# Weight sums moved from Pool to VectorE, one tile's statistics to ScalarE, transposes ahead of loads, in a fused attention and GLU kernel

## Chip, cores, metric

The kernel runs on one core of a Trainium2 chip. The metric is device time in microseconds (us) for one execution; a time quoted for a kernel is the median of its runs. Runs of one kernel lie within about 0.3% of each other. The comparisons below use five rounds, and the trace of one profiled run of each kernel to see where time went. In the views PE is TensorE (matmuls), PEld its weight loads, DVE VectorE, ACT ScalarE, POOL Pool and SPq the queue that issues transfers; a bank is a part of PSUM, the memory that TensorE writes its results to, and PEclk or granted clock is the share of its full clock that TensorE was given.

## The reference, cut to what matters

```python
h  = x + A_ref(layernorm(x), wqkv, wo)      # linear attention, S=2048, D=1024, 32 heads
h2 = h + B_ref(layernorm(h), W_gate, W_up, W_down)   # gate*relu-mask*up, F=3584
# A_ref: q, k, v = x @ wqkv;  phi(t) = where(t > 0, t + 1, exp(t)) + 1e-6
#        kv = sum_s phi(k) v;  o = phi(q) kv / (phi(q) z);  return o @ wo
```

Only the first 125 us of the kernel matter here: layer norm of x and the products for k, v and q.

## The kernel before

The rows of x come in 16 tiles of 128. Each is normalized, transposed (tiles 0 to 3 on TensorE, later ones by DMA) and multiplied with the weights. From the tiles 0 and 1 on for keys, and from tiles 6 and 7 on for values, a pair of tiles is multiplied by a Strassen-like scheme with seven products instead of eight. It needs sums of weight blocks (`w_sums`, four per matrix, computed once) and sums of x blocks (`x_sums`, four per pair of tiles). The first values are plain products (`v_piece`). A queue of each engine is filled in program order by `PL.add`, with semaphores worked out from buffers read and written.

```python
def x_sums(p):                       # four 512-column sums per pair of tiles, VectorE
    ...
    add(2, xb(0, 0), xb(0, 1), ALU.subtract, ...)      # read by product P7, the second one
    add(0, xb(0, 1), xb(1, 1), ALU.add, ...)
    add(1, s(0), xb(0, 0), ALU.subtract, ...)          # read by P6, the third one
    add(3, xb(1, 0), s(1), ALU.subtract, ...)

# start of the program, tiles 1 to 5 (cut)
v_piece(0, 0, lambda: T1(1))         # T1(t): the eight TensorE transposes of tile t
v_piece(1, 0, lambda: T1(2))
x_sums(0)
ln1_norm(3)
pool_q += w_sums("pool", wv_, bw_v, tw_v, B_TWv, "TWv", 1, NW // 2)    # values: 32 pieces
v_piece(2, 0, lambda: T1(3))
v_piece(0, 1)
twk = w_sums("dve", wkv, bw_k, tw_k, B_TWk, "TWk", KH)                 # keys: 4 sums
...
pool_q += w_sums("pool", wq, bw_q, TWq, B_TWq, "TWq", 1, NW // 2)      # queries: 32 pieces
...
# hooks of a key group: pieces of Pool work, statistics of the tiles to come
def k1():
    pool_piece(2)
    if A < NST:
        ln1_stats(A)                 # VectorE
def k5():
    pool_piece(2)
    if B < NST:
        m_, q_ = ln1_stats_act(B)    # ScalarE
        ...
# the group of seven products, in the order of TensorE (cut)
#   P1, P7 (x sum 3), P6 (x sum 2), P2, P5 (x sum 1), P4, P3 (x sum 4); ScalarE copies a bank
#   after P1 (needed by P6) and after P6 (needed by P5), VectorE and ScalarE finish the results
```

In the profiles L804 of the kernel before (L800 after) is `w_sums`, L829 (L825) `x_sums`, L739 (L733) and L673 norms, L688, L691 and L907 (L903) the finishing of keys, L616 every matmul, L754 (L748) the transposes on TensorE, L630 to L637 statistics on VectorE, L654 and L659 statistics on ScalarE, L640 and L662 to L668 the norms' small root steps on Pool.

## Time and profile before

| | before |
|---|---|
| time, median of the runs made with the prediction's result | 751.87 us |
| TensorE busy | 739.3 us (99%) |
| VectorE busy | 538.4 us (72%) |
| Pool busy | 89.9 us (12%) |
| TensorE time lost, 12 to 15 us | 0.92 us |
| TensorE time lost, 43.5 to 53 us | 3.49 us |

"Time lost" is worked out from the trace: the distance between the starts of consecutive matmuls, less 0.213 us for 512 columns (in proportion for fewer); the median distance is 0.216 us, so a little of every matmul counts as lost. Some traces lack 56 of the 3,595 matmul records; a missing record looks like 0.213 to 0.219 us lost, and I took those out, but not in the half-clock stretches below, where each matmul loses 0.213 us and none is missing (as many matmuls as weight loads). The first 12 us are left out of comparisons, because their loss ranged from 2.8 to 4.2 us between profiled runs with the arrival of the first loads.

The page of the kernel before, busy time by engine and Pool's busy tenths in 40 slices of the span:

```profile
PE 739.3 (99%) x3595; PEld 335.1 (45%) x3595; DVE 538.4 (72%) x1063; ACT 308.0 (41%) x532; POOL 89.9 (12%) x152
...
POOL 2985620000360000000000010000000000000000
```

TensorE is the bound, so only its idle time can be won. The chain for tile 3, from the timeline of the kernel before (start, duration, engine, line; in brackets the idle time before and who ended it):

```profile
12.21 0.75 DVE L829 TENSOR_TENSOR RWG<-RAB 128x512 f16<-128x512 bf16 x2
...
13.80 0.54 DVE L673 TENSOR_SCALAR RXH<-RE,mv,rstd 128x1024 bf16<-128x1024 bf16 x1
14.39 0.45 PEld L754 LDWEIGHTS ps<-ident,RXH 128*128 128x128 bf16 x8 [1.22 <-DVE RXH L673]
14.39 0.62 PE L754 MATMUL ps<-ident,RXH 128*128 128x128 bf16 x8 [0.73 <-DVE RXH L673]
```

The norm L673 stands behind the x sums L829, and TensorE waits for it. The larger loss, from VectorE's and Pool's timelines of the kernel before:

```profile
25.59 8.21 POOL L804 TENSOR_TENSOR RW<-RAB 128x256 f16<-128x256 bf16 x10
...
38.02 10.87 POOL L804 TENSOR_TENSOR RW<-RAB,RW 128x256 f16<-128x256 bf16 x14
```

```profile
34.60 0.76 DVE L688 TENSOR_SCALAR RX<-RX 128x512 bf16<-128x512 bf16 x1
...
41.43 0.78 DVE L829 TENSOR_TENSOR RWG<-RWG,RAB 128x512 f16<-128x512 f16 x1
42.24 0.77 DVE L829 TENSOR_TENSOR RH<-RAB,RWG 128x512 f16<-128x512 bf16 x1
42.94 1.27 DVE L630 BATCH_NORM_STATS2 st<-RE 128x6 f32<-128x512 bf16 x2
...
47.02 1.34 DVE L829 TENSOR_TENSOR RWG<-RAB 128x512 f16<-128x512 bf16 x2
48.40 0.77 DVE L829 TENSOR_TENSOR RWG<-RWG,RAB 128x512 f16<-128x512 f16 x1
```

The wait itself, from the timeline of the kernel before:

```profile
47.70 1.02 PE L616 MATMUL ps<-RW,RWG 128*128 128x512 f16 x4 [2.20 <-DVE RWG L829]
```

And the waits view of the kernel before for 40 to 50 us (who waited for whom, us in total, times, longest):

```profile
PEld ps L616 <- POOL RW L804: 2.7, 1, 2.7
PE ps L616 <- DVE RWG L829: 2.2, 1, 2.2
```

The view names two culprits for one gap, before the second product of the first value group. The Pool sum that this product reads is the first of the four, 8 of the 32 pieces, and four pieces ran before the ten shown from 25.59 us; the eighth ended near 29 us. The x sum, the other operand, started at 47.02 us. So the question is why VectorE was late; its operations beside Pool's take 0.76 to 0.78 us where 0.29 (L688) and 0.42 us (L829) are their usual times.

### The profile page before, as it was taken

The page shows a single profiled execution, that of the slowest core. Times are in us where ns is not written, and L with a number is a line of the kernel's source. Part 1 is how long each engine was busy: PE and PEld are TensorE (multiplying, and loading weights), DVE is VectorE, ACT ScalarE, POOL GpSimd, SP SyncE. Part 2 cuts the span into 40 slices and gives each one's busy share as a digit, 9 for nine tenths or more (in the row PEclk, how much of TensorE's full clock was granted, in tenths as well). Part 3 has the DMA queues.
Part 4 walks back from the last instruction along what each step waited for, and adds up shares of the span by engine and source line. Part 5 has one row for each costly group of instructions (what it writes and reads, how often), then busy time and mean ns, then how long its engine had stood idle before and what let it go on. Part 6 is the DMA issues. An engine that isn't in the chain of part 4 may idle for free.

```text
span 750.0 us, 10163 instructions
## 1 busy us (share of the span) xinstructions
PE 739.3 (99%) x3595; PEld 335.1 (45%) x3595; DVE 538.4 (72%) x1063; ACT 308.0 (41%) x532; POOL 89.9 (12%) x152
## 2 busy tenths in 40 slices
PE   8989999999999999999999999999999999999998
PEld 3434444344554444444444444444444444444443
DVE  7797856889776799888877494856868677563343
ACT  4657755664842354545453100035454454520000
POOL 2985620000360000000000010000000000000000
PEclk9999999999999999999999999999999999999999
DMA  9624135013998796665537799733324241035764
GB/s 303 201 58 113 28 97 165 35 22 66 218 224 238 218 302 191 176 180 173 158 97 234 193 292 301 246 110 98 92 78 111 59 112 56 1 85 182 210 189 134
DMA packets 160226, 113.39 MB, mean 151 GB/s; under 512 B 51504, under 2 KB 141360, under 8 KB 160176
## 3 DMA queue, kind: packets, MB, share of 16 engines
q1 hardware_dynamic: 160176, 112.75, 53.4%
q8 instruction: 28, 0.46, 0.2%
q14 instruction: 22, 0.18, 0.1%
HBM read 85.46 MB, written 15.73 MB: 135 GB/s over the span
## 4 chain that ended last, share of the span: by engine, by line
PE 87%; DVE 6%; ACT 3%; issue 2%; DMA 1%; SPq 1%; DVEq 0%; POOL 0%; ACTq 0%
PE ps L616 87%; DVE RAB L691 1%; ACT ps L621 1%; DMA RE<-in_A_x_dram 1%; DVE RX L688 1%; ACT RXH L654 1%; ACT RXH L659 1%; SPq L522 1%; DVE RE L1062 1%; DVE RX L907 0%; ACT RX L684 0%; ACT RX L621 0%; DVE RWG L829 0%; DVE RE L691 0%; DMA RW<-in_B_W_down_dram 0%
## 5 line engine op out<-in xcount | busy, mean ns | idle before, releaser
L621 ACT ACTIVATE ps<-ps 128x512 f32<-128x512 f32 x154 | 89.7, 583 | 182.1 <-PE ps L616 163.3
L616 PE MATMUL ps<-RC,RO 128*128 128x512 f16 x672 | 154.5, 379 | 0.5 <-DVE RE L1243 0.4
L616 PE MATMUL ps<-RW,RAB 128*128 128x512 f16 (+1 forms) x692 | 150.8, 379 | 0.0
L616 PE MATMUL ps<-RH,RWG 128*128 128x512 bf16 x448 | 106.0, 379 | 0.3 <-DVE RAB L1236 0.3
L616 PEld LDWEIGHTS ps<-RW,RAB 128*128 128x128 bf16 (+1 forms) x692 | 67.7, 98 | 81.7
L621 ACT ACTIVATE RE<-ps 128x512 f32<-128x512 f32 x120 | 70.7, 597 | 75.1 <-PE ps L616 52.8
L616 PEld LDWEIGHTS ps<-RC,RO 128*128 128x128 f16 x672 | 65.5, 98 | 80.5 <-ACT ps L621 1.1
L616 PE MATMUL ps<-RC,RWG 128*128 128x512 f16 x320 | 76.6, 380 | 0.1
L616 PEld LDWEIGHTS ps<-RH,RWG 128*128 128x128 bf16 x448 | 43.7, 98 | 53.4 <-DVE RAB L1236 0.8
L1236 DVE TENSOR_TENSOR RAB<-ps,RAB 128x512 bf16<-128x512 f32 x28 | 19.3, 690 | 63.8 <-PE ps L616 63.8
L616 PE MATMUL ps<-RH,RO 128*128 128x512 bf16 (+1 forms) x256 | 61.2, 379 | 0.0
L621 ACT ACTIVATE RAB<-ps 128x512 bf16<-128x512 f32 x56 | 33.4, 597 | 61.9 <-PE ps L616 61.8
L616 PE MATMUL ps<-RW,RE 128*128 128x512 bf16 x256 | 57.4, 379 | 0.4 <-DVE RXH L1086 0.4
L616 PE MATMUL ps<-RAB 128*128 128x512 bf16 x200 | 48.1, 379 | 0.1
L616 PEld LDWEIGHTS ps<-RC,RWG 128*128 128x128 bf16 (+1 forms) x320 | 30.0, 98 | 39.9 <-ACT ps L621 5.9
L1167 DVE TENSOR_TENSOR RO<-RWG,RO 128x512 f16<-128x512 bf16 x108 | 45.5, 421 | 1.8
L1167 DVE TENSOR_TENSOR RO<-RWG 128x512 f16<-128x512 bf16 x108 | 40.7, 418 | 3.2 <-DMA RWG<-in_B_W_up_dram 2.3
L1243 DVE TENSOR_TENSOR RE<-ps,RE 128x512 f32<-128x512 f32 x56 | 38.2, 690 | 4.7 <-ACT RE L621 4.7
L640 POOL TENSOR_TENSOR rstd<-rstd,neghalf 128x1 f32<-128x1 f32 x18 | 11.6, 647 | 249.1 <-DVE rstd L637 249.1
L1248 DVE TENSOR_TENSOR RE<-ps,RE 128x512 f32<-128x512 f32 x56 | 38.2, 682 | 0.0
L616 PEld LDWEIGHTS ps<-RH,RO 128*128 128x128 f16 (+1 forms) x256 | 24.6, 98 | 29.4 <-ACT RX L621 1.1
L616 PEld LDWEIGHTS ps<-RW,RE 128*128 128x128 bf16 x256 | 24.5, 98 | 28.0 <-DVE RXH L1086 0.7
(118 smaller groups left out, 817.1 us busy)
## 6 DMA issues: line engine op xcount, KB each, us to landing
RWG<-in_B_W_gate_dram SPq DMA_DIRECT2D x28, 512.0 KB, 4.0
RWG<-in_B_W_up_dram SPq DMA_DIRECT2D x28, 512.0 KB, 5.0
RW<-t_scr SPq DMA_DIRECT2D x56, 256.0 KB, 3.2
RW<-in_B_W_down_dram SPq DMA_DIRECT2D x42, 256.0 KB, 4.3
RW<-in_B_W_down_dram SPq DMA_DIRECT2D x14, 512.0 KB, 3.9
t_scr<-RW SPq DMA_DIRECT2D x14, 512.0 KB, 4.8
RE<-in_A_x_dram SPq DMA_DIRECT2D x23, 256.0 KB, 3.2
RAB<-in_A_wqkv_dram SPq DMA_DIRECT2D x8, 512.0 KB, 8.2
```

The lines of the kernel that those rows point to most:

```text
L522: return PL.add("sp", lambda e: e.dma_start(dst_ap, src_ap), reads=reads, writes=writes, slot=slot, name=name)
L616: lambda e: e.matmul(out_ap, lhsT, rhs, start=start, stop=stop, skip_group_check=skip),
L621: PL.add("act", lambda e: e.activation(out=dst, in_=src, func=func), reads=reads, writes=writes, name=name)
L640: PL.add("pool", lambda e: e.tensor_tensor(out=rstd[:, k, :], in0=rstd[:, k, :], in1=neghalf[:], op=ALU.pow), reads=[B_neghalf], writes=[B ...
L654: PL.add("act", lambda e: e.activation(out=junk, in_=src, func=ACTF.Identity, scale=1.0 / D, accum_out=sv[:, 0:1]), reads=src_bufs, writes ...
L659: PL.add("act", lambda e: e.activation(out=junk, in_=src, func=ACTF.Square, scale=float(D) ** -0.5, accum_out=sv[:, 1:2]), reads=src_bufs, ...
L688: PL.add("dve", lambda e: e.tensor_scalar(out=Et[:, k, :], in0=Et[:, k, :], scalar1=1.0, scalar2=1e-6, op0=ALU.min, op1=ALU.add), reads=[] ...
L691: PL.add("dve", lambda e: e.scalar_tensor_tensor(out=dst_ap, in0=src, scalar=C1, in1=Et[:, k, :], op0=ALU.add, op1=ALU.max), reads=[src_bu ...
L1167: PL.add(eng, lambda e: e.tensor_tensor(out=Tring[:, k, j], in0=in0, in1=in1, op=ALU.subtract), reads=reads, writes=[B_T[k][j]], name="T%d ...
L1236: PL.add("dve", lambda e: e.tensor_tensor(out=hh[:, f1, 0:SBW], in0=bank(BA[1]), in1=r11[:, rr, :], op=ALU.mult), reads=[B_bank[BA[1]], B_ ...
L1243: PL.add("dve", lambda e, w=w: e.tensor_tensor(out=ftmp[:, 4 + w, :], in0=bank(BF_[w]), in1=ftmp[:, 2 + w, :], op=ALU.add), reads=[B_bank[ ...
L1248: PL.add("dve", lambda e, w=w: e.tensor_tensor(out=ftmp[:, 6 + w, :], in0=bank(BB[w]), in1=ftmp[:, w, :], op=ALU.add), reads=[B_bank[BB[w] ...
```

## The change

The intent: take the sums of value and query weights off Pool, do them on VectorE where it is idle, move the statistics of tile 6 from VectorE to ScalarE in exchange, put tile 3's norm ahead of the first x sums with its transposes half a value piece later, and issue the DMA transpose of a tile ahead of the next x load. The edit also takes tile 5's statistics on ScalarE two value pieces earlier (`m5`, `q5`, not in the cut). The diff, cut to its core:

```diff
-            if 6 <= st + NX1 < NST:
+            if st in (2, 3):
                 load_x1(st + NX1)
@@ def T1d(st):
             dma_t(sl_tx[k], xnT[:, :, st * P:(st + 1) * P], xn[:, k, :], ...)
+            if st + NX1 < NST:
+                load_x1(st + NX1)
@@
+        twk = w_sums(wkv, bw_k, tw_k, B_TWk, "TWk", KH)
+        twv = w_sums(wv_, bw_v, tw_v, B_TWv, "TWv", KH)          # 4 sums of 2048 columns, VectorE
+        twq = w_sums(wq, bw_q, TWq, B_TWq, "TWq", KH // 2)       # 8 sums of 1024 columns, VectorE
         v_piece(0, 0, lambda: T1(1))
         v_piece(1, 0, lambda: T1(2))
-        x_sums(0)
         ln1_norm(3)
-        pool_q += w_sums("pool", wv_, bw_v, tw_v, B_TWv, "TWv", 1, NW // 2)
-        v_piece(2, 0, lambda: T1(3))
-        v_piece(0, 1)
+        x_sums(0)
+        v_piece(2, 0)
+        twv.pop(0)()
+        v_piece(0, 1, lambda: T1(3))
 ...
+        m6, q6 = ln1_stats_act(6)          # tile 6 on ScalarE, between copies of value pieces
+        m6()
+        twk.pop(0)()
+        v_piece(2, 1)
+        q6()
+        twv.pop(0)()
+        twk.pop(0)()
+        twv.pop(0)()
         v_piece(3, 1)
 ...
             def k1():
-                pool_piece(2)
-                if A < NST:
+                if p > 0 and A < NST:
                     ln1_stats(A)
+                for _ in range(nq[0]):
+                    twq.pop(0)()
 ...
         norms(3)
+        twv.pop(0)()
 ...
+        NQ = {2: (0, 1), 3: (0, 1), 4: (0, 1), 5: (2, 2), 6: (1, 0)}   # where query sums go
```

## The prediction

> **What bounds the kernel.** TensorE: the page gives PE 739.3 of 750.0 us busy (99%), DVE 72%, ACT 41%, Pool 12%, granted clock 1.0. A change pays only by the TensorE idle time it closes. From the starts of consecutive matmuls in the trace, counting what exceeds 0.213 us for 512 columns, the run loses 23 us. The change touches only 12 to 125 us, where three losses are above 0.5 us:
> - 0.89 us before 14.39 us: the transposes of tile 3 wait for its norm on DVE (timeline), because the four sums of x (L829, 12.21 to 13.87 us) stand ahead of it in DVE's queue.
> - 2.37 us before 47.70 us, then 0.71 us before 49.27 us: the first value group of seven products. The waits view charges 2.66 us to Pool's sum into RW and 2.20 us to DVE L829. The Pool sum this product reads was among the first 8 of 32 pieces, done near 29 us; the real releaser is L829 (x sums, from 47.02 us). DVE is behind: 23.4 of 25 us busy from 25 to 50 us.
>
> **Why DVE is behind.** Beside Pool's 256-element pieces (0.67 us each, back to back from 38.0 to 48.9 us) its operations stretch: L688 0.29 to 0.77 us, L829 0.42 to 0.77, L691 0.69 to 1.11. The Trainium skill, SBUF — State Buffer, "SBUF: two separate sides", says VectorE and GpSimd share a port pair, held for a whole instruction, the loser blocking; this trace agrees. I add up about 3.5 us of stretching from 33 to 47 us.
>
> **What changes.** Pool loses 64 pieces (12.7+11.3 us values, 23.4 us queries). DVE gains 4 operations of 2048 columns (1.22 us as measured for key sums, 1.69 us in the form with an fp16 operand) and 8 of 1024 columns (estimate 0.6 to 0.85 us): about 5.5 and 5.8 us. Tile 6's statistics leave DVE (1.6 us) for ScalarE (2.3 us). Three value sums run at 15 to 27 us, the fourth after the norms of tiles 6 and 7. Tile 3's norm goes ahead of the x sums, its transposes half a value piece later.
>
> **On the critical path.**
> - Tile-3 wait: closed, -0.9 us.
> - First value group: before 45 us DVE loses 1.6 us of statistics and 3 to 4 us of stretching and gains 1.2 us, so the x sums should be ready in time: -3.1 us.
> - New risk at the first key group (24 to 28 us): two statistics passes interleave with copies at 1.73 us per pair against 1.71 us of PE per piece, so ScalarE's first bank copy may be late: +0.3 us.
> - Query sums fill DVE idle time at 60 to 110 us: 0. From 125 us on only start times move; the gains carry through.
>
> **Prediction.** 752.2 - 0.9 - 3.1 + 0.3 = 748.5 us; 746.7 to 750.4 should hold it 8 times in 10. Faster by over 2%: 0.01; within 2%: 0.98; slower by over 2%: 0.01.
>
> **What would show it.** No PE gap above 0.3 us at 13 to 16 us, none above 0.5 us at 44 to 50 us; Pool busy near 43 us instead of 89.9; L829 and L688 near 0.42 and 0.29 us throughout; DVE busy up by 4 to 8 us; about 4 us earlier start of every stage from 52 us on.
>
> **What would make it wrong.** DVE blocked in order by tile 5's norm (which waits for ScalarE and Pool), so that key sums come late; ScalarE late at the first key group; or the gap at 47 us ruled by the arrival of transposed tiles, not DVE.

## The result, and the profile after

The changed kernel took 747.79 us (four runs, 747.65 to 747.97) against 751.87 us of the kernel before. The ratio is 0.9945, with a 95% interval of 0.9928 to 0.9962; a second set of five rounds, listed among the experiments, gave 0.9938 (0.9924 to 0.9951). A ratio here is the mean time of one kernel's fast runs over that of the other's of the same rounds, so it is not quite the ratio of the medians quoted. Where I compare two variants with each other, I use their ratios to the kernel before.

| | before | after |
|---|---|---|
| TensorE time lost, 12 to 15 us | 0.92 | 0.03 |
| lost, 15 to 43.5 us | 0.55 | 0.54 |
| lost, 43.5 to 53 us | 3.49 | 0.56 |
| lost, 53 to 130 us | 4.11 | 4.26 |
| Pool busy | 89.9 | 43.9 |
| VectorE busy | 538.4 | 536.7 |
| span of the profiled run | 750.0 | 746.0 |

The two closed gaps, 0.89 + 2.93 = 3.82 us, are nearly the whole 4.0 us between the spans. The page after:

```profile
PE 736.1 (99%) x3539; PEld 336.0 (45%) x3595; DVE 536.7 (72%) x1071; ACT 309.7 (42%) x536; POOL 43.9 (6%) x90
...
POOL 2411000001350000000000010000000000000000
```

(Its 3,539 matmuls are the case of missing matmul records; weight loads are complete.) The timeline after, for tile 3:

```profile
12.77 0.55 DVE L673 TENSOR_SCALAR RXH<-RE,mv,rstd 128x1024 bf16<-128x1024 bf16 x1 [0.66 <-POOL rstd L640]
13.23 0.75 DVE L825 TENSOR_TENSOR RWG<-RAB 128x512 f16<-128x512 bf16 x2
...
15.19 0.61 PE L748 MATMUL ps<-ident,RXH 128*128 128x128 bf16 x8
```

No wait stands in brackets before the transposes any more. The first value group:

```profile
43.84 0.76 DVE L825 TENSOR_TENSOR RWG<-RAB 128x512 f16<-128x512 bf16 x2
44.32 0.60 PEld L616 LDWEIGHTS ps<-RW,RWG 128*128 128x128 f16 x4 [0.26 <-DVE RWG L825]
44.39 2.00 PE L616 MATMUL ps<-RW,RWG 128*128 128x512 f16 x8
44.63 0.42 DVE L825 TENSOR_TENSOR RWG<-RWG,RAB 128x512 f16<-128x512 f16 x1
```

The x sums start at 43.84 us, not at 47.02, and are at their usual 0.38 us for one of the pair and 0.42. TensorE hardly waits, but note the small wait on L825: VectorE is only just in time. Pool and VectorE meet in one more place, where Pool now loses (timeline after):

```profile
22.23 5.16 POOL L662 TENSOR_SCALAR s<-s 128x1 f32<-128x1 f32 x1 [0.67 <-ACT RXH L654]
...
22.59 1.22 DVE L800 TENSOR_TENSOR RC<-RAB,RC 128x2048 f16<-128x2048 bf16 x1
...
23.72 1.22 DVE L800 TENSOR_TENSOR RW<-RAB 128x2048 f16<-128x2048 bf16 x1
...
25.99 1.22 DVE L800 TENSOR_TENSOR RW<-RAB,RW 128x2048 f16<-128x2048 bf16 x1
```

A Pool step on one column, 0.30 us elsewhere, lasted 5.16 us and ended when VectorE's run of weight sums did. It delays tile 6's norm inputs to about 28.4 us; the norm runs at 36 us, so nothing waits for it. In a second profiled run of the same kernel (after2) the step took 1.62 us.

### The profile page after: what moved, and what is told of

The parts are those of the page before. It is cut to its first block, busy times and chain, and to the rows that moved or that the text cites. A ratio compares the mean times of both kernels' runs of the same rounds, so it can differ in the third digit from the quotient of the medians.

```text
span 746.0 us, 10031 instructions
## 1 busy us (share of the span) xinstructions
PE 736.1 (99%) x3539; PEld 336.0 (45%) x3595; DVE 536.7 (72%) x1071; ACT 309.7 (42%) x536; POOL 43.9 (6%) x90
## 4 chain that ended last, share of the span: by engine, by line
PE 88%; DVE 5%; ACT 4%; issue 2%; DMA 0%; SPq 0%; DVEq 0%; POOL 0%; ACTq 0%; POOLq 0%
PE ps L616 88%; DVE RAB L691 1%; ACT ps L621 1%; ACT RX L684 1%; DVE RE L1058 1%; DVE RX L688 1%; ACT RXH L654 1%; ACT RXH L659 1%; ACT RX L621 1%; DVE RX L903 0%; DMA RW<-in_B_W_down_dram 0%; SPq L522 0%; DVE RXH L1082 0%; PE ps L748 0%; DVE RE L691 0%
## 5 line engine op out<-in xcount | busy, mean ns | idle before, releaser
L616 PE MATMUL ps<-RH,RWG 128*128 128x512 bf16 x435 | 103.2, 379 | 1.0 <-DVE RAB L1232 0.3
L616 PE MATMUL ps<-RH,RO 128*128 128x512 bf16 (+1 forms) x242 | 58.3, 379 | 0.7
L688 DVE TENSOR_SCALAR RX<-RX 128x512 bf16<-128x512 bf16 x64 | 18.6, 290 | 22.8 <-ACT RX L684 22.7
```

Of the source, the lines that this page charges most:

```text
L616: lambda e: e.matmul(out_ap, lhsT, rhs, start=start, stop=stop, skip_group_check=skip),
L688: PL.add("dve", lambda e: e.tensor_scalar(out=Et[:, k, :], in0=Et[:, k, :], scalar1=1.0, scalar2=1e-6, op0=ALU.min, op1=ALU.add), reads=[] ...
```

## Experiments

Theory: the gain is the order of tile 3 (0.9 us) plus VectorE freed of Pool's interference (about 3 us). Rivals: Pool's value sums themselves came late, as the waits view says; the relief is the moved statistics; Pool's queue delays the small steps of the norms; the transposes arrive earlier. Twelve kernels ran; all gave correct results.

### Undoing or doing one part

**b_norm3**: the kernel before with only tile 3's order changed.

```diff
-        x_sums(0)
         ln1_norm(3)
+        x_sums(0)
-        v_piece(2, 0, lambda: T1(3))
-        v_piece(0, 1)
+        v_piece(2, 0)
+        v_piece(0, 1, lambda: T1(3))
```

> The kernel before, with only the order of tile 3 changed: its norm ahead of the sums of x on VectorE, its transposes half a value piece later. My theory: the 0.89 us loss at 13 us closes and nothing else moves, so 0.7 to 1.0 us faster than before (about 751.0 against 751.9), with the loss of about 2.4 us at 44 us still there. Rival (order does not matter, the later wait absorbs it because the stage at 47 us is set by Pool or VectorE work and not by TensorE): 0 gain, and the loss at 44 us grows to about 3.2 us.

Measured 752.36 us against 752.25 for the kernel before, ratio 1.0001 (0.9988 to 1.0013). The trace shows the loss at 12 to 15 us closed (0.03 us), but 0.45 us more lost at 24 to 30 us, where the first key group's sixth product waits, and the loss from 43.5 us on still there (4.4 us, of which 1.3 us is explained below by the clock). So the expected 0.7 to 1.0 us did not come, nor did the gap grow to 3.2 us as the rival said. Part was given back at 28 us, the rest is inside the noise of the first 12 us and of the clock. At 28 us TensorE waits for a key sum on VectorE. Before that sum VectorE had stood 2.63 us in front of tile 5's norm (L739), whose root step on Pool came after ScalarE's statistics of tile 5 (timeline of this run):

```profile
26.61 0.88 DVE L739 TENSOR_SCALAR RXH<-RE,s 128x1024 bf16<-128x1024 bf16 x1 [2.63 <-POOL s L668]
...
29.16 1.04 PE L616 MATMUL ps<-RC,RAB 128*128 128x512 f16 x4 [0.29 <-DVE RC L804]
```

By itself, this part is inconclusive.

**a_norm3undo**: the changed kernel with this order put back (the reverse of the diff above).

> The changed kernel with tile 3's norm and transposes put back where they were before. In the kernel before this order alone gained nothing clear of noise, since VectorE ruled at 28 and 44 us; in the changed kernel VectorE has room, so my theory expects the 0.9 us loss at 13 us to come back in full: 0.6 to 1.0 us slower than the changed kernel. Rival (the order is worth nothing anywhere): within 0.2 us of it.

Measured 748.91 us, ratio 0.9953 (0.9942 to 0.9965), against 0.9938 and 0.9945 for the changed kernel: 0.6 to 1.1 us slower (0.0008 to 0.0015 of 752 us). Its trace loses 0.92 us at 12 to 15 us and nothing new elsewhere after that. With VectorE relieved, and with tile 5's statistics earlier, so that the wait of 2.63 us is gone, the order is worth what its gap was; the intervals overlap, so the trace is the firmer evidence.

**b_act6**: the kernel before with the statistics of tile 6 on ScalarE, but put where that kernel leaves room, around the last value piece.

```diff
         twk.pop(0)()
+        m6, q6 = ln1_stats_act(6)
+        m6()
         v_piece(3, 1)
+        q6()
...
-                if A < NST:
+                if p > 0 and A < NST:
                     ln1_stats(A)
```

> The kernel before, with only the statistics of tile 6 moved from VectorE (28 to 29.8 us) to ScalarE. My prediction counted these 1.6 us as relief before 45 us. Looking again, VectorE waits for ScalarE's exponentials at about 32 us, so the relief may be lost there: my theory as revised expects 0 to 0.4 us gain. Rival (the statistics are what puts VectorE behind): 1.3 to 1.7 us gain, the loss at 44 us down to about 0.8 us.

Measured 753.91 us, ratio 1.0024 (1.0011 to 1.0036): slower. My placement was bad: it puts a second pair of passes in front of the bank copy of the first key group. TensorE in the timeline of this run:

```profile
27.37 0.82 PE L616 MATMUL ps<-RC,RWG 128*128 128x512 f16 x3 [1.32 <-ACT ps L621]
```

The loss at 24 to 30 us rose from 0.12 to 1.54 us, and the one from 43.5 to 53 us was 4.1 us, of which 1.2 us is half clock (below); without that it fell only from 3.49 to about 3.0 us. Moving the statistics did not close the gap, but because of the new stall this run doesn't measure their worth cleanly; the next one does.

**a_stats6**: the changed kernel with tile 6's statistics back on VectorE (`m6`, `q6` removed, `if A < NST` restored).

> The changed kernel with the statistics of tile 6 back on VectorE in the first key group. There VectorE waits 1.4 us for ScalarE's exponentials at 31 us, so I expect the 1.6 us to be absorbed: 0 to 0.4 us slower than the changed kernel. Rival (my prediction's term: 1.6 us of the relief is this): about 1.3 to 1.6 us slower, seen as a loss at 44 us.

Measured 748.09 us, ratio 0.9941 (0.9929 to 0.9954), the same as the changed kernel; loss from 43.5 to 53 us 0.56 us, also the same. The statistics run where VectorE waits for ScalarE's exponentials anyway; in the changed kernel that wait is 1.39 us (timeline after):

```profile
31.30 0.29 DVE L688 TENSOR_SCALAR RX<-RX 128x512 bf16<-128x512 bf16 x1 [1.39 <-ACT RX L684]
```

This part of the change gained nothing, and the 1.6 us that my prediction counted as relief were none.

**a_qpool**: the changed kernel with the query sums in 32 Pool pieces again, two per hook of groups 2 to 5.

> The changed kernel with the query sums back on Pool, 32 pieces between 51 and 105 us. VectorE has spare time there, so stretching costs nothing on TensorE: within 0.3 us of the changed kernel, Pool busy about 67 us. Rival (any Pool work beside VectorE costs): 1 us or more slower.

Measured 747.83 us, ratio 0.9938 (0.9926 to 0.995): no difference. Moving the query sums gained nothing.

**only_v**: a_qpool, a_stats6 and a_norm3undo together; what is left are value sums on VectorE, the order of transposes and loads, and the earlier place of tile 5's statistics. By 32 us that place no longer matters: VectorE's operation L691 starts at 32.57 us before and 31.62 us after, as far apart as TensorE's plain products before it (30.44 and 29.49 us).

> Of the changed kernel only the value sums on VectorE and the transposes issued ahead of loads are kept; query sums on Pool, statistics of tile 6 on VectorE, tile 3 in the old order. My theory: the losses at 44 to 50 us close by this alone, about 3 us faster than before, 0.9 us slower than the changed kernel. Rival (VectorE takes on 4.9 us of sums in its busiest stretch, so it needs the statistics moved as well): less than 2 us faster than before, with a loss over 1 us at 44 us.

Measured 748.63 us, ratio 0.995 (0.9937 to 0.9963). The loss from 43.5 to 53 us is 0.56 us as in the changed kernel, the one at 12 to 15 us 0.80 us. So the value sums close the large gap without the other parts, although VectorE takes on four sums of 1.22 us in its busy stretch.

**a_load**: the changed kernel with each x load ahead of the transpose again.

> The changed kernel with the load of the next x tile issued ahead of the transpose again, as before. The loads are needed some 13 us later and the transposes by the next group, so both theories that I have expect 0 within 0.3 us; a loss above 0.5 us would mean that the transposes' arrival, not VectorE, ruled the first value group.

Measured 747.92 us, ratio 0.9939 (0.9927 to 0.9952), beside 747.93 us for the changed kernel (after2). No effect. The arrival of the transposes did not rule the gap in the kernel before either: tile 7's was issued at 41.33 us and such a transfer landed after 3.5 us at the median, 2 us before the x sums began at 47.02 us.

**after2**: the changed kernel again.

> The changed kernel once more, unaltered, as the yardstick for the other runs of this call: 747.5 to 748.2 us, about 4 us faster than before.

Measured 747.93 us (747.6 to 748.1), ratio 0.9938. As expected.

### Interference or lateness

**a_dead**: the changed kernel with 32 Pool subtractions added, at the places where the kernel before had its value sums; nobody reads their result.

```diff
+        def dead_pieces():
+            def go(dc, c0, r, dep):
+                PL.add("pool", lambda e: e.tensor_tensor(out=dead[:], in0=wv_[:, dc, c0:c0 + 256],
+                                                         in1=wv_[:, dc, NW + c0:NW + c0 + 256], op=ALU.subtract),
+                       reads=[B_wkv[2][0], B_wkv[3][0]], writes=[B_dead], deps=[dep], name="dead")
```

> The changed kernel, plus 32 Pool subtractions of 256 columns at the places where the kernel before had its value sums; they read the value weights, write a buffer that nobody reads, so no result waits for them. My theory (Pool stretches VectorE's operations and so the x sums of the first value group come late): the loss at 44 us comes back, 1.5 to 3 us, about 749.3 to 750.8 us in all, with L688 and the x sums stretched to 0.77 us. Rival (the gain came from the value sums themselves being ready earlier, as the waits view of before says of Pool's RW): no change, 747.8 us.

Measured 756.38 us, ratio 1.0054 (1.0041 to 1.0066): over 8 us slower than the changed kernel, and the loss before the first value group is 6.3 us. So the work on Pool does the harm without any result being waited for; the rival of late value sums is out. The size is two to four times what I expected; VectorE also keeps its own value sums here, so this is not the kernel before restored. VectorE's timeline of this run (lines are shifted: L690 is L688 of before, L749 is L739, L816 weight sums, L841 x sums):

```profile
28.15 1.69 DVE L816 TENSOR_TENSOR RW<-RAB,RW 128x2048 f16<-128x2048 bf16 x1
29.76 0.76 DVE L690 TENSOR_SCALAR RX<-RX 128x512 bf16<-128x512 bf16 x1
...
40.94 0.88 DVE L749 TENSOR_SCALAR RXH<-RE,s 128x1024 bf16<-128x1024 bf16 x1 [2.51 <-POOL s L670]
...
45.09 0.77 DVE L841 TENSOR_TENSOR RWG<-RWG,RAB 128x512 f16<-128x512 f16 x1
```

Weight sums went from 1.22 to 1.69 us, x sums from 0.42 to 0.77. There is a second mechanism too, which I had not counted: VectorE stood 2.51 us in front of a norm whose root step (L670) was queued on Pool behind dead pieces. The kernel before has no wait for Pool on VectorE from 33 to 51 us, so this mechanism had no part in the gap that the change closed. And the clock adds to it (below).

**a_deadms**: the same, but the dead operations are fills of 640 columns, about 0.7 us each, which read nothing.

```diff
-                PL.add("pool", lambda e: e.tensor_tensor(out=dead[:], in0=..., in1=..., op=ALU.subtract), ...)
+                PL.add("pool", lambda e: e.memset(dead[:], 0.0), writes=[B_dead], deps=[dep], name="dead")
```

> As a_dead, but the 32 dead Pool operations are fills of 640 columns, which keep Pool busy about as long (0.65 us each) and read nothing. If what hurts is the shared SBUF port, operations of VectorE with two SBUF inputs (the x sums) stay at 0.42 us, and at most the one-input L688 stretches: loss at 44 us 0 to 0.8 us, total within 1 us of 747.8. Rival (what hurts is Pool's queue, which delays the small reciprocal-root steps of the norms, or Pool being busy at all): the same loss as a_dead.

Measured 748.55 us, ratio 0.995 (0.9937 to 0.9964), 0.4 to 0.9 us slower than the changed kernel; the loss before the value group is 1.1 us. Pool was as busy from 20 to 50 us as in a_dead (27.0 and 27.4 us). VectorE's timeline (L815 weight sums, L840 x sums):

```profile
27.25 1.21 DVE L815 TENSOR_TENSOR RW<-RAB,RW 128x2048 f16<-128x2048 bf16 x1
...
31.83 0.83 DVE L690 TENSOR_SCALAR RX<-RX 128x512 bf16<-128x512 bf16 x1 [1.13 <-ACT RX L686]
...
40.71 0.43 DVE L840 TENSOR_TENSOR RWG<-RWG,RAB 128x512 f16<-128x512 f16 x1
```

Operations with two inputs in SBUF keep their usual times beside fills, while the one-input L690 stretches from 0.29 to 0.83 us. This is what the Trainium skill says, page SBUF — State Buffer, section "Who interferes with whom": "A DVE instruction with two SBUF inputs contends with a GpSimd instruction that reads SBUF, not with one that only writes it", and that operations in a two-port mode contend with GpSimd (Pool) as well; that L690 ran in such a mode is not shown by a run. So it is Pool's reading of SBUF, not its being busy, that stretched the sums.

### Two tries for more

**a_wd**: in the changed kernel, VectorE stands 4.23 us in front of down-weight sums (L602) whose load has not landed; the view names no releaser, but the load's last semaphore update in the trace is at 244.39 us (timeline after):

```profile
244.47 1.56 DVE L602 TENSOR_TENSOR RW<-RW 128x512 f16<-128x512 bf16 x4 [4.23 <-issue]
245.95 0.68 DVE L1232 TENSOR_TENSOR RAB<-ps,RAB 128x512 bf16<-128x512 f32 x1
```

```diff
-        wt_at = {0: [0], 1: [1, 2], 2: [3, 4]}
-        for q in range(3, 12):
+        wt_at = {1: [0, 1], 2: [2, 3], 3: [4, 5]}
+        for q in range(4, 12):
```

> A try at a further gain: the changed kernel with the down-weight sums of the first pair moved to the second pair, so that VectorE does not stand 4.2 us in front of a weight load that has not landed (244 us). The three TensorE losses of 0.46, 0.52 and 0.33 us at 245 to 250 us should close: 1.0 to 1.4 us faster than the changed kernel, if the doubled sums in the second pair do not make VectorE late in turn.

Measured 746.22 us (four runs, 745.91 to 746.67), ratio 0.9916 (0.9902 to 0.9929). The loss at 238 to 260 us fell from 1.58 us (after2) to 0.26 us. VectorE's timeline now has the bank work first:

```profile
240.81 0.69 DVE L1232 TENSOR_TENSOR RAB<-ps,RAB 128x512 bf16<-128x512 f32 x1 [0.31 <-PE ps L616]
...
249.75 2.55 DVE L602 TENSOR_TENSOR RW<-RW 128x512 f16<-128x512 bf16 x7
```

This is the fastest version: 1.7 us below the changed kernel by medians, of which the trace shows 1.3. The gain is a little more than the 1.0 to 1.4 us expected.

**a_wdh**: a_wd, and in each group of seven products the held-back exponentials behind the second bank copy.

```diff
-            hook(2)
             c = alloc_bank(pool)
             prod(b, SX(1), TW(1), False, "P6")
             ident_act(bank(c), bank(b), [B_bank[b]], [B_bank[c]], name + "fk2")
+            hook(2)
             hook(3)
```

> a_wd, and in each group of seven products the held-back exponentials go behind ScalarE's second bank copy instead of ahead of it. The loss of 0.26 us at the fifth product of each of the five value groups and the first query group should close: 1.0 to 1.5 us faster than a_wd, 2 to 2.9 us faster than the changed kernel.

Measured 750.21 us, ratio 0.9969 (0.9956 to 0.9981): 4 us slower than a_wd. The 0.26 us losses at the fifth product are gone, but what came later is late now: from TensorE's timeline of this run, the accumulation of keys and values waits for the finished keys:

```profile
117.59 0.64 PE L616 MATMUL ps<-RE 128*128 128x129 bf16 x8 [1.01 <-DVE RE L691]
```

Five more waits of 0.31 us of this kind stand in the groups before it, and 0.36 to 0.48 us ones in the query groups. ScalarE's exponentials, now behind its copy, made the finished keys and queries late: a wait that was closed became larger waits further on.

### The clock, which nobody asked about

In b_norm3 the granted clock dropped for one stretch. The windows view of that run (the stretch; then its length, and busy us with instruction counts of PE, PEld, DVE, ACT and POOL; then PEclk, DMA share, GB/s):

```profile
45.57:48.98 3.41, 1.25 (x6) 0.32 (x4) 3.34 (x7) 1.73 (x4) 3.10 (x5) 1.00 0.01 2
48.98:52.39 3.41, 2.90 (x8) 1.05 (x8) 3.31 (x6) 1.55 (x3) 3.25 (x6) 0.50 0.02 5
```

After a stretch with TensorE 1.25 of 3.41 us busy, the clock was halved for the next 3.41 us, and seven matmuls there lost about 1.3 us. The same followed a stretch of 1.12 of 3.41 us busy in b_act6, and of 0.77 of 3.42 us in a_dead. The profiled run of the kernel before kept clock 1.00 (1.88 of 3.42 us busy from 43.62 to 47.04 us). Of the 29 runs of the kernel before, 19 report a mean clock of 0.998 and average 752.7 us; 10 report 1.0 and average 751.8 us. The changed kernel's runs in after2 all report 1.0 (three of the first four 0.999; the one profiled drops only in its last 1.4 us, after the last matmul). So the gap at 44 us probably cost more than itself in most runs: an estimate from these averages is 0.9 us × 19/29 = 0.6 us on the mean. That this is the same event in each of those 19 runs is argued from the mean clock; only profiled runs show the place. In a_dead the same happened for 6.8 us.

## Why the prediction was right

- **Bound and gaps.** It named the two places and sizes, 0.9 and 3.1 us. The trace shows 0.89 and 2.93 us closed. Sum predicted 752.2 to 748.5 us, measured 751.87 to 747.79 us.
- **Not Pool's lateness.** Against the waits view, it held VectorE's x sums as the releaser and Pool as the cause of their lateness. a_dead shows the harm with no one waiting for Pool's results, a_deadms shows that it needs Pool to read SBUF.
- **Terms that were mis-sized or wrong.** "before 45 us DVE loses 1.6 us of statistics" was true and worth nothing (a_stats6). "ScalarE's first bank copy may be late: +0.3 us" measured 0: loss 24 to 30 us 0.12 before, 0.11 after; b_act6 shows that the danger was real, with 1.32 us of idle time in one wait for that copy. "DVE busy up by 4 to 8 us" was wrong: it fell by 1.7 us. The new sums took 4 × 1.22 + 8 × 0.69 = 10.4 us (I had costed 11.3), the statistics left with 1.6 us, so about 10.5 us of stretching went away, of which I had counted only the part from 33 to 47 us. The 1.69 us form of a weight sum, which I took for its own cost, was itself stretched; it runs at 1.22 us after, and the norm L739 at 0.54 instead of 0.89 us.
- **Some luck.** Without the 1.6 us of statistics my own sum leaves 1.8 to 2.8 us of relief, against 2.37 us at the larger wait. That it was enough is close to luck: VectorE is only just in time after.
- **Additivity.** I added the two gains. In the changed kernel they do add (a_norm3undo, only_v), but the first does not pay in the kernel before (b_norm3), where VectorE is late at 28 us as soon as TensorE comes earlier. I had named this danger, VectorE held in order by tile 5's norm, for the changed kernel; it was the kernel before that had it.
- **Query sums, order of loads.** Predicted 0 for the first, measured 0 (a_qpool); the second, not costed, is 0 (a_load).
- **Missing term.** The half-clock stretch that the gap seems to trigger in many runs. It may be why later rounds put the gain at 0.62% rather than the 0.5% forecast, though the intervals hold both; the two profiled runs, neither of which has such a stretch at 44 us, show 3.8 us, close to the prediction's 3.7.

## What to carry to other kernels

Before believing that an engine is busy, compare one operation's duration in the crowded stretch with its duration elsewhere: work given to an "idle" Pool can make VectorE late although nothing waits for Pool. When a wait names two releasers, check when each operand was really finished. And test parts in both directions: a part that gains nothing alone may be worth its full gap once the engine behind it has room, and a wait that is closed by reordering one queue may open a larger one at the next result of that queue.

## What the Trainium skill lacked or had wrong

- SBUF — State Buffer, section "Who interferes with whom": it says that whoever issues first holds the shared ports for the whole instruction. It doesn't say that a waiting Pool instruction can lose against a whole run of VectorE instructions: here a step of 0.30 us took 5.16 us beside VectorE's run of 1.22 us sums, and ended 0.18 us after the last of them (27.39 and 27.21 us); in after2, the same kernel, it took 1.62 us and ended after the first. That it waited for the ports all this time is inferred from these times. In the other direction VectorE's sums lost 0.35 to 0.47 us each beside back-to-back Pool pieces of about 0.67 us, less than one piece.
- TensorE: Matmul & The Clock Gate, section "What's actually happening": it gives half clock "after ≥1 idle window (~3.4µs)". The window of 3.41 us agrees with the traces. The page gives no share of busy time below which such a window counts as idle, and it need not be idle throughout: in b_norm3 the longest distance between the starts of two matmuls was 2.5 us, TensorE was busy 1.25 of 3.41 us, and the clock was still halved for the next 3.41 us; with 1.88 of 3.42 us busy (kernel before) it was not.
